# Batch 0 of a fused attention and gated MLP kernel in another order: loads, conversion, gate, outputs and attention parts

## Chip, cores, metric

One core of a Trainium2 chip. The metric is device time in microseconds (us), median of several executions. The engines are TensorE (PE), VectorE (DVE), ScalarE (ACT), and SyncE, which issues most of the DMAs.

## The reference

```python
# attention: x (8,8,512,64), state (8,8,32,64), float32, per batch and head
scores = x @ state.T / 8;  a  = softmax(scores);   xread = a @ state    # tokens read the state
scores2 = state @ x.T / 8; a2 = softmax(scores2);  sread = a2 @ x       # the state reads the tokens
# bridge: (batch, head, 544, 64) -> (4352, 512), then
h = x @ w_in             # w_in (512, 2048), float64 in memory
g = h * cos(h)
out = g @ w_out          # w_out (2048, 512), float64 in memory
```

## The kernel before

The weights come as float64 and are converted to float32 on the chip: 18 loads, each through two steps on DVE (`convert1`), two on ACT, two on DVE (`convert2`) and one on DVE (`convert3`). This happens in batch 0, beside its work. Later batches have nothing to convert.

For the tokens, `a @ state @ w_in` is regrouped. `products` computes state x w_in for a block of 512 columns (`sw`), and a tile's "hidden" matmul is `sw` x `aT` (128 of the 2048 columns for 512 tokens). The gate is a copy with a rounding bias (ACT), a subtraction (DVE), Abs and Sin (ACT) and a product (DVE). The "output" matmuls accumulate g x w_out in four PSUM tiles; the line `line` keeps them some tiles behind. All attention parts go through one PSUM tile, `at`. The schedule is manual: each engine gets its instructions in program order.

```python
st_src = state.rearrange("b (k j) n d -> j k n b d", j=2)
for k in range(NK):
    for j in range(2):
        queue = nc.sync if j == 0 else nc.scalar
        queue.dma_start(out=st[Ns * k:Ns * k + Ns, :, D * j:D * j + D], in_=st_src[j, k])
# ... (cut) weights: first 512 columns of w_in, then w_in and w_out in turn
for a, b in zip(rest_in, rest_out):
    loads += [a, b]
# ... (cut)
load_x(0); fetch(3); states()              # states(): turn the state on PE, copy on ACT and DVE
a0 = attn[0] = Attention(0)
a0.all_tokens(); a0.scores()               # turn x on PE, copy; scores into `at`
# ... (cut) softmax of batch 0 with the first two conversions between
for t in tiles(b):                         # 16 tiles a batch; conv = 3 + t.f in batch 0
    hidden(t)
    gate(t)                                # ACT q <- h
    if conv and t.f: convert1(conv + 1)
    gate2(t)                               # DVE q <- q, h
    if conv: convert2(conv)                # (first tile cut)
    gate3(t)                               # ACT Abs, Sin
    go()                                   # one attention part, if the slot has one
    line.append(t)
    if len(line) > 3: output(line.pop(0))
    gate4(t)                               # DVE g <- h, q
    if conv: convert3(conv)
    go()
```

## Time and profile before

| | before |
|---|---|
| median (first three runs) | 903.25 us |
| PE busy | 841.5 us, 93% of the span |
| PE without a gap | from 178.1 us (batch 1's first hidden matmul) |
| hidden 0 starts | 29.20 us |

From 178 us on PE has no hole.

### The profile page before, as it was taken

How to read it: one execution, taken by the hardware profiler on the slowest of the kernel's cores; microseconds unless marked ns; L12 is line 12 of the kernel's file. 1: busy time of each engine (PE TensorE's matmuls, PEld its weight loads, DVE VectorE, ACT ScalarE, POOL GpSimd, SP SyncE). 2: the span in 40 equal slices, each digit the busy share in tenths (PEclk: the TensorE clock that was granted, in tenths of full speed). 3: DMA queues.
4: the chain of work that ended last, by engine and by line, in shares of the span. 5: the costliest groups of instructions: out<-in, count | busy, mean ns of one | idle time of the engine just before them, and what ended most of it. 6: DMA issues, size and time to landing. Idle time of an engine off the chain costs nothing.

```text
span 901.1 us, 7084 instructions
## 1 busy us (share of the span) xinstructions
PE 841.5 (93%) x2720; PEld 385.2 (43%) x2720; DVE 356.7 (40%) x520; ACT 408.9 (45%) x631; POOL 0.7 (0%) x6
## 2 busy tenths in 40 slices
PE   3569867899999999999999999999999999999997
PEld 2134324244534453444444443445344534444664
DVE  4687885335322443245224522353225322222121
ACT  2546563355344634464344525453455344434332
POOL 0000000000000000000000000000000000000000
PEclk9689988999999999999999999999999999999999
DMA  6632630021000300030003000300010000000100
GB/s 163 186 141 96 184 140 1 0 70 24 1 1 23 71 0 1 1 93 1 0 1 93 1 0 1 91 4 1 1 47 1 0 1 23 24 0 1 47 1 23
DMA packets 45377, 35.05 MB, mean 39 GB/s; under 512 B 36384, under 2 KB 36384, under 8 KB 45344
## 3 DMA queue, kind: packets, MB, share of 16 engines
q1 hardware_dynamic: 44256, 34.35, 13.4%
q8 instruction: 21, 0.34, 0.2%
q10 hardware_dynamic: 1088, 0.26, 0.2%
q14 instruction: 12, 0.10, 0.0%
HBM read 25.69 MB, written 8.91 MB: 38 GB/s over the span
## 4 chain that ended last, share of the span: by engine, by line
PE 86%; DVE 7%; ACT 4%; issue 1%; DMA 0%; ACTq 0%; DVEq 0%
PE o L403 48%; PE h L373 28%; PE at L245 5%; PE at L311 3%; PE at L219 1%; DVE e L176 1%; ACT e L165 1%; ACT raw L166 1%; DVE w_in L189 1%; PE at L300 1%; DVE w_in L179 1%; ACT q L379 1%; ACT q L388 1%; DVE w_out L189 1%; DVE q L382 1%
## 5 line engine op out<-in xcount | busy, mean ns | idle before, releaser
L403 PE MATMUL o<-w_out,g 128*128 128x512 f32 x1088 | 495.3, 597 | 5.9 <-DVE w_out L189 5.9
L403 PEld LDWEIGHTS o<-w_out,g 128*128 128x128 f32 x1088 | 204.4, 192 | 249.3 <-issue 236.7
L373 PE MATMUL h<-aT,sw 128*128 128x512 f32 x512 | 250.9, 613 | 4.1 <-ACT sw L343 3.4
L382 DVE SCALAR_TENSOR_TENSOR q<-q,h 128x512 f32<-128x512 f32 (+1 forms) x144 | 94.3, 655 | 348.0 <-ACT q L379 348.0
L379 ACT ACTIVATE q<-h 128x512 f32<-128x512 f32 (+1 forms) x144 | 82.5, 573 | 276.1 <-PE h L373 276.1
L393 DVE TENSOR_TENSOR g<-h,q 128x512 f32<-128x512 f32 (+1 forms) x144 | 95.2, 661 | 158.9 <-ACT q L388 158.7
L373 PEld LDWEIGHTS h<-aT,sw 128*128 128x128 f32 x512 | 96.4, 195 | 128.3 <-issue 111.2
L387 ACT ACTIVATE q<-q 128x512 f32<-128x512 f32 (+1 forms) x144 | 87.2, 606 | 105.2 <-DVE q L382 105.2
L388 ACT ACTIVATE q<-q,halfpi 128x512 f32<-128x512 f32 (+1 forms) x144 | 100.5, 698 | 4.5
L245 PE MATMUL at<-w_in,stT 64*32 64x512 f32 (+1 forms) x528 | 41.6, 606 | 24.1 <-DVE w_in L189 12.2
L343 ACT COPY sw<-at 128x1024 f32<-128x1024 f32 (+1 forms) x33 | 32.3, 978 | 43.6 <-PE at L245 43.6
L311 PE MATMUL at<-x_b,a2T 128*128 128x256 f32 x128 | 32.0, 396 | 4.0 <-DVE a2T L303 4.0
L311 PEld LDWEIGHTS at<-x_b,a2T 128*128 128x128 f32 x128 | 25.3, 199 | 13.9 <-issue 6.5
L373 PE MATMUL h<-sT,w_in 128*128 128x256 f32 x128 | 30.2, 379 | 0.0
L245 PEld LDWEIGHTS at<-w_in,stT 64*32 64x32 f32 x528 | 6.8, 106 | 54.8 <-DVE w_in L189 17.8
L373 PEld LDWEIGHTS h<-sT,w_in 128*128 128x128 f32 x128 | 24.3, 190 | 10.1 <-issue 5.0
L409 ACT ACTIVATE ot<-o 128x512 f32<-128x512 f32 x34 | 19.4, 596 | 19.8 <-DMA out_dram<-ot 14.7
L165 ACT ACTIVATE e<-e,ebias 128x1024 int32<-128x1024 int32 (+1 forms) x18 | 18.9, 1051 | 11.4 <-DVE e L162 11.4
L219 PEld LDWEIGHTS at<-ident,x_b 128*128 128x128 f32 x112 | 13.8, 141 | 16.7 <-issue 12.0
L263 DVE STREAM_TRANSPOSE spread<-m 128x1024 f32<-128x1024 f32 x16 | 19.8, 1236 | 0.0
L176 DVE SCALAR_TENSOR_TENSOR e<-raw,e 128x1024 int32<-128x1024 int32 (+1 forms) x18 | 19.7, 1096 | 0.0
L226 ACT COPY xT<-at 128x512 f32<-128x512 f32 x28 | 16.0, 571 | 8.1 <-PE at L219 8.1
(49 smaller groups left out, 269.5 us busy)
## 6 DMA issues: line engine op xcount, KB each, us to landing
x_b<-in_x_dram SPq DMA_DIRECT2D x32, 256.0 KB, 4.7
raw<-in_moe_w_out_dram SPq DMA_DIRECT2D x8, 1024.0 KB, 4.8
out_dram<-ot SPq DMA_DIRECT2D x32, 256.0 KB, 2.2
raw<-in_moe_w_in_dram SPq DMA_DIRECT2D x6, 1024.0 KB, 5.2
raw<-in_moe_w_in_dram SPq DMA_DIRECT2D x4, 512.0 KB, 5.4
out_dram<-ot SPq DMA_DIRECT2D x8, 64.0 KB, 1.7
st<-in_state_dram ACTq DMA_DIRECT2D x4, 64.0 KB, 3.2
st<-in_state_dram SPq DMA_DIRECT2D x4, 64.0 KB, 3.0
```

Source lines behind the costliest of these rows:

```text
L165: nc.scalar.activation(e, e, func=ACTF.Relu, bias=ebias, scale=8.0)
L176: nc.vector.scalar_tensor_tensor(out=e, in0=raw[:, :, :, 1], scalar=-2 ** 31, in1=e, op0=ALU.bitwise_and, op1=ALU.bitwise_or)
L245: nc.tensor.matmul(out=at[Ns * k:Ns * k + Ns, j, 0:n], lhsT=w[D * j:D * j + D, self.b, Ns * k:Ns * k + Ns], rhs=r(slice(D * j, D * j + D), k),
L311: nc.tensor.matmul(out=at[:, 0, cols], lhsT=self.a2T[:, j, c, :], rhs=self.x_b[:, c].rearrange("p (k j) d -> p j k d", j=2)[:, j], start=( ...
L343: nc.scalar.copy(sw_of[self.b, nt][:, :, c0:c1], at[:, :, 0:c1 - c0])
L373: nc.tensor.matmul(out=t.hp, lhsT=t.lhs(i), rhs=t.rhs(i), start=(i == 0), stop=(i == t.kn - 1))
L379: nc.scalar.activation(t.q, t.hp, func=ACTF.Copy, bias=MAGIC)
L382: nc.vector.scalar_tensor_tensor(out=t.q, in0=t.q, scalar=MAGIC, in1=t.hp, op0=ALU.subtract, op1=ALU.subtract)
L387: nc.scalar.activation(t.q, t.q, func=ACTF.Abs)
L388: nc.scalar.activation(t.q, t.q, func=ACTF.Sin, bias=halfpi, scale=-TWO_PI)
L393: nc.vector.tensor_tensor(t.g[:, 0:t.n], t.hp, t.q, op=ALU.mult)
L403: nc.tensor.matmul(out=acc[i], lhsT=t.g[:, P * i:P * i + P], rhs=w_out[:, t.f, :], start=(t.f == 0), stop=(t.f == NF - 1))
```

## The change

The intent: let PE, which waits through most of batch 0, wait less. x's loads go first. w_in is converted ahead of w_out, so that each block of `products` is ready a tile earlier. Conversion steps go ahead of the gate within a tile. Outputs run four tiles behind. The parts by which the state reads the tokens (turns, reads) go into the middle slots, and three of batch 1's four product sets go into batch 1.

```diff
-    queue = nc.sync if j == 0 else nc.scalar
-    queue.dma_start(out=st[...], in_=st_src[j, k])
+    nc.scalar.dma_start(out=st[...], in_=st_src[j, k])      # after load_x(0) on nc.sync
@@ loads
-    for a, b in zip(rest_in, rest_out):
+    for a, b in zip(rest_in[1:], rest_out):                 # rest_in[0] put right behind the first four
@@ turn
-            nc.vector.tensor_copy(a2T[:, j], at[:, j])
+            nc.scalar.copy(a2T[:, j], at[:, j])
@@ start
-    states(); a0.all_tokens(); a0.scores()
+    a0.all_tokens(); states(); a0.scores()
     (exp2 and max2 behind norm1; the first products into output tiles instead of `at`)
@@ batch 0's slots (two a tile; P0, P1 products, L state half, E softmax half of batch 0 or 1)
+    slots0 = [[], [P0[0]], E1[0:1], E1[1:2], E1[2:3], E1[3:4], [P0[1]],
+              L0[0:1], L0[1:2], [], L0[2:3], L0[3:4], L0[4:5], [],
+              [P0[2]], L0[5:6], E1[4:5], E1[5:6], E1[6:7], E1[7:8], E1[8:9],
+              E1[9:10], [P0[3]], E1[10:11], E1[11:12], L1[0:1],
+              L1[1:2], [P1[0]], L1[2:3], L1[3:4], L1[4:5], L1[5:6]]
@@ tile
             hidden(t)
-            gate(t)
             if conv and t.f:
                 convert1(conv + 1)
+                convert2(conv)
+            gate(t)
             gate2(t)
-            if conv: convert2(conv)
+            if conv: convert3(conv)
             gate3(t)
             ...
-            if len(line) > 3:
+            if len(line) > 4:
                 output(line.pop(0))
             gate4(t)
-            if conv: convert3(conv)
```

(The g buffers grow from five to six.)

More of the change, by code (lines that the diff above doesn't have):

```diff
@@ L53 @@
     swp = ctx.enter_context(tc.tile_pool(name="swp", bufs=6))
-    gp = ctx.enter_context(tc.tile_pool(name="gp", bufs=5))
+    gp = ctx.enter_context(tc.tile_pool(name="gp", bufs=6))
     msb = ctx.enter_context(tc.tile_pool(name="msb", bufs=2))
@@ L76, with load_x @@
     make_identity(nc, ident)
+    x_t = {}
+    def load_x(b):
+        x_b = xin.tile([P, NC, H, D], F32, name="x_b")
+        src = x[b].rearrange("h (c p) d -> c p h d", p=P)
+        for c in range(NC):
+            nc.sync.dma_start(out=x_b[:, c], in_=src[c])
+        x_t[b] = x_b
+    load_x(0)
     st_src = state.rearrange("b (k j) n d -> j k n b d", j=2)
@@ L79 @@
         for j in range(2):
-            queue = nc.sync if j == 0 else nc.scalar
-            queue.dma_start(out=st[Ns * k:Ns * k + Ns, :, D * j:D * j + D],
-                            in_=st_src[j, k])
+            nc.scalar.dma_start(
+                out=st[Ns * k:Ns * k + Ns, :, D * j:D * j + D],
+                in_=st_src[j, k])
     at = aps.tile([P, 2, S], F32, name="at")
@@ L96, in states @@
                                     op0=ALU.mult)
-    x_t = {}
-    def load_x(b):
-        x_b = xin.tile([P, NC, H, D], F32, name="x_b")
-        src = x[b].rearrange("h (c p) d -> c p h d", p=P)
-        for c in range(NC):
-            nc.sync.dma_start(out=x_b[:, c], in_=src[c])
-        x_t[b] = x_b
     w_in = consts.tile([P, NK, Dff], F32)
@@ L129 @@
     rest_out = [out_load(f) for f in range(0, NF, 2)]
-    for a, b in zip(rest_in, rest_out):
+    for a, b in zip(rest_in[1:], rest_out):
         loads += [a, b]
-    loads += rest_out[len(rest_in):]
+    loads.insert(len(loads) - 2 * (len(rest_in) - 1), rest_in[0])
+    loads += rest_out[len(rest_in) - 1:]
     raws = {}
@@ L238, in all_tokens, with per_head @@
                     nc.vector.tensor_copy(self.xT[:, k], xp[k])
-        def per_head(self, w, r, n=S):
+        def per_head(self, w, r, n=S, to=None):
             for k in range(NK):
@@ L245, in per_head @@
                     nc.tensor.matmul(
-                        out=at[Ns * k:Ns * k + Ns, j, 0:n],
+                        out=(to[j] if to else at[:, j])[Ns * k:Ns * k + Ns,
+                                                        0:n],
                         lhsT=w[D * j:D * j + D, self.b, Ns * k:Ns * k + Ns],
@@ L276, in shift, with exp1, exp2 @@
             nc.vector.tensor_tensor(self.z1, at, self.spread, op=ALU.subtract)
-        def exps(self):
+        def exp1(self):
             nc.scalar.activation(self.z1, self.z1, func=ACTF.Exp)
+        def exp2(self):
             for j in range(2):
@@ L283, in exps @@
                                      accum_out=self.i2[:, j:j + 1])
+        def exps(self):
+            self.exp1()
+            self.exp2()
         def inverse(self, v):
@@ L302, in turn @@
                                     identity=ident)
-            nc.vector.tensor_copy(
-                self.a2T[:, j].rearrange("p c m -> p (c m)"), at[:, j])
+            nc.scalar.copy(self.a2T[:, j].rearrange("p c m -> p (c m)"),
+                           at[:, j])
         def reads(self, j):
@@ L343, in products, with first_products @@
             nc.scalar.copy(sw_of[self.b, nt][:, :, c0:c1], at[:, :, 0:c1 - c0])
+        def first_products(self, n):
+            to = [ops.tile([P, Dm], F32, name="o") for j in range(2)]
+            self.per_head(stT, lambda rows, k: w_in[rows, k, 0:n], n, to)
+            sw_of[self.b, 0] = swp.tile([P, 2, WC], F32, name="sw")
+            for j in range(2):
+                nc.scalar.copy(sw_of[self.b, 0][:, j, 0:n], to[j][:, 0:n])
         def scores1(self):
@@ L440, in tiles @@
             yield t
-    load_x(0)
     fetch(3)
-    states()
     a0 = attn[0] = Attention(0)
     a0.all_tokens()
+    states()
     a0.scores()
@@ L450 @@
     a0.max1()
+    a0.spread1()
+    a0.shift()
+    a0.exp1()
     convert2(0)
     convert3(0)
-    a0.spread1()
-    a0.shift()
-    a0.max2()
-    a0.exps()
+    a0.sums()
     convert1(1)
-    a0.sums()
     a0.spread1()
@@ L462 @@
     a0.norm1()
+    a0.first_products(HC)
+    a0.max2()
+    a0.exp2()
     load_x(1)
-    a0.products(0, 0, HC)
     convert1(2)
     convert1(3)
-    first = [lambda: a0.products(0, HC, WC)] + parts(0, PRODS[1:])
+    P0 = [lambda: a0.products(0, HC, WC)] + parts(0, PRODS[1:])
+    L0 = parts(0, LATE)
+    W1 = parts(1)
+    E1, L1, P1 = W1[:12], W1[12:18], W1[18:]
+    slots0 = [[], [P0[0]], E1[0:1], E1[1:2], E1[2:3], E1[3:4], [P0[1]],
[3 more added lines that the diff above has]
+              L1[1:2], [P1[0]], L1[2:3], L1[3:4], L1[4:5], L1[5:6]]
     line = []
@@ L471 @@
         work = parts(b + 1) if b + 1 < B else []
-        if b == 0:
-            late = parts(0, LATE)
-            work = ([None] + first[:1] + late[:5] + first[1:2] + late[5:]
-                    + work[:4] + [None] * 2 + first[2:3] + work[4:11]
-                    + first[3:] + work[11:])
-        n_slots, slot = 2 * NF, 0
-        n_done = 0
+        if b == 1:
+            work = P1[1:] + work
+        n_slots, slot, n_done = 2 * NF, 0, 0
         def go():
             nonlocal n_done, slot
+            if b == 0:
+                for part in slots0[slot]:
+                    part()
             slot += 1
             want = (len(work) * slot + n_slots - 1) // n_slots
-            if b == 0:
-                n = 3 * NF // 2
-                want = min(slot, n) + max(slot - n, 0) * (len(work) - n) // (
-                    n_slots - n)
-            while n_done < want:
-                if work[n_done]:
-                    work[n_done]()
+            while n_done < want and b > 0:
+                work[n_done]()
                 n_done += 1
@@ L508 @@
                     convert3(conv - 1)
-                convert2(conv)
+                    convert2(conv)
+                convert3(conv)
             gate3(t)
@@ L512 @@
             line.append(t)
-            if len(line) > 3:
+            if len(line) > 4:
                 output(line.pop(0))
             gate4(t)
-            if conv:
-                convert3(conv)
-                if t.f == 0:
-                    convert1(conv + 1)
+            if conv and t.f == 0:
+                convert1(conv + 1)
             go()
```

## The prediction

> **What bounds the kernel now.** I read the page's 40 slices first. TensorE (PE) is at 9 from slice 10 on; it is only in the first eight slices (22.5 us each, batch 0) that it is not.
>
> ```profile
> PE   3569867899999999999999999999999999999997
> ...
> DVE  4687885335322443245224522353225322222121
> ACT  2546563355344634464344525453455344434332
> ...
> PEclk9689988999999999999999999999999999999999
> ```
>
> Then the table of windows. To be seen: from 180 us on PE has no gap until the last microseconds, so the end is "when does PE become gapless" plus "how much matmul work is left then". Before that VectorE (DVE), which converts the weights from f64, is the fullest engine.
>
> ```profile
> 20.00:30.00 10.00, 2.96 (x17) 0.90 (x18) 9.70 (x16) 5.10 (x10) 0.00 (x0) 0.50 0.23 70
> 140.00:150.00 10.00, 4.42 (x17) 2.61 (x16) 10.00 (x13) 4.69 (x6) 0.00 (x0) 0.81 0.01 2
> 180.00:190.00 10.00, 10.00 (x34) 5.12 (x33) 2.76 (x4) 5.42 (x9) 0.00 (x0) 1.00 0.01 2
> 280.00:500.00 220.00, 220.00 (x717) 98.03 (x716) 78.06 (x112) 104.61 (x164) 0.00 (x0) 1.00 0.12 29
> ```
>
> Third, the chain in order of time, for one tile of batch 0. To be seen: ACT holds the gate's first copy (L379), then two conversion steps, then Abs and Sin, then the attention's copy; only then may PE transpose and run the next tile's "hidden" matmul. That loop is 6.8 us while a settled tile needs 1.72 (L373 x4) + 3.44 (L403 x8) = 5.16 us.
>
> ```profile
> 78.16 0.60 ACT q L379
> 78.76 1.04 ACT e L165
> 79.79 1.05 ACT raw L166
> 80.84 0.53 ACT q L387
> 81.39 0.72 ACT q L388
> 82.11 0.48 ACT xT L226
> 82.64 0.66 PE at L219 x4
> 83.30 1.73 PE h L373 x4
> ```
>
> Last, PE's waits: no single one is large, so no single removal can give much. (The chain names the rest: round trips between DVE, ACT and PE.)
>
> ```profile
> PE at L245 <- DVE w_in L189: 12.2, 6, 3.3
> PE at L245 <- ACT z L281: 8.3, 1, 8.3
> PE o L403 <- DVE w_out L189: 5.9, 4, 4.6
> PE at L300 <- DVE a2T L303: 5.2, 2, 3.7
> PE at L311 <- DVE a2T L303: 4.0, 1, 4.0
> ```
>
> **How much is lost now.** Batch 1's first hidden matmul starts at 178.1 us (timeline). Done by then, at warm durations: 16 hidden x 1.72 = 27.5; 13 outputs x 3.44 = 44.7; attention of batches 0 and 1, from its own rows (a set of products or scores 1.1, reads of one batch 3.4, turns 0.9, 16 transposes of x 1.8), about 25.3. Sum 97.5. So some 80.6 us are lost, 29.2 minus about 4 of them before tile 0. At most this can be won, and DVE's work forbids most of it.
>
> **What the Trainium skill says.** "TensorE: Matmul & The Clock Gate", Part 1: PE idles at half rate, and about 3.4 us of activity releases it. The trace agrees: granted clock 0.50 at 20 to 30 us, and the first hidden matmul takes 3.79 us against 1.72 later. The same page's note on queue depths calls ACT and DVE strict FIFO. The trace agrees: the z transposes at 43.30 end near 44.1, but their 0.6 us copy on DVE (L303) starts only at 47.05, behind the gate and two conversion steps. "ScalarE: Activation LUTs", section on ACT_TABLE_LOAD: about 1283 ns for a switch of set, plus a drain. The trace has the 1.28 us load; no 1.38 us drain is to be seen, the next activation follows at once.
>
> **The change, part by part.**
>
> *Start.* x now leads its queue (issued near 0.7 instead of 3.45 us), but state and x still share the DMA engines, which were full until about 10 us, and the state's two transpose halves come after x's copies on ACT and DVE. By trace durations the scores start at about 13.4 to 14.8 us (13.04 now). From there the order on DVE is shorter: max 1.25, spread 1.2, shift 1.23, conversion 0 1.83, sums 1.87, half of conversion 1 0.66, spread 1.25, conversion 1 1.83, so the first products can go 13.1 us after the scores, their copies end at 15.0, and hidden 0 starts 15.05 after the scores; now it is 29.20 - 13.04 = 16.16. Together 28.5 to 29.8 us: nothing won.
>
> *Order in a tile.* Now ACT runs L379, L165, L166, L387, L388; after, the two conversion steps come ahead of L379. Worked through from the start of a tile's first DVE step (pitches from the timeline: L162 and L163 0.6 each, L176, L179, L189 1.14 each, L382 and L393 0.6): ACT starts e at 0.73, raw ends 2.83, L379 until 3.45; DVE has finished its two conversion steps at 3.5, gate2 to 4.1, last conversion step to 5.25; ACT's Sin starts at 4.89, so gate4 runs 5.64 to 6.25. Period 6.25 us, DVE waiting only 0.4 of it. Attention pieces on DVE add to this.
>
> *w_in ahead of w_out.* Columns 512 to 1023 are ready after tile 2 instead of tile 3, the next two sets after 6 and 10. The products then stand in the first slot of tiles 3, 7, 11, beside the gate, and the 12.2 us of waits on L189 should go. The next hidden matmul still waits for ACT's 1.0 us copy of them.
>
> *Tiles 0 to 3.* With output delayed to four tiles, PE does nothing there but hidden matmuls and x's transposes of batch 1, so it stays mostly cold (3.4 us each). ACT's copy after Sin, transpose, copy and cold hidden make tiles 2 and 3 about 7.5 us. By this walk gate4 ends at 38.4, 47.3, 54.8, 62.3 us for tiles 0 to 3; now 38.1, 48.3, 56.2, 63.9. Little won.
>
> *Tiles 4 to 13.* Here it gains. DVE's work: 10 tiles x 5.94 (conversion 4.65 + gate 1.29) = 59.4, keep 1.5, batch 1's softmax 9.0 (1.25 + 1.14 + 1.15 + 1.21 + 1.8 + 1.24 + 1.22), sum 69.9. Waits on top: 0.4 in most tiles, 3; a cold hidden 4 behind turn 0, 2; tile 5, where PE has 8.6 us (hidden, two halves of reads, output), 2; Exp's table load ahead of the sums with no conversion step left to fill the gap, 2. So gate4 of tile 13 ends near 62.3 + 69.9 + 9 = 141 us (now 149). a2T's copies move from DVE to ACT right behind Sin, which removes most of the L303 waits (9.2 us).
>
> *From there.* PE is gapless from batch 1's first products, placed after tile 13's Sin, about 140.5 us. Done by then: 14 hidden 24.1 + 10 outputs 34.4 + attention 17.3 (as above, without batch 1's reads 3.4, three product sets 3.3 and small parts) = 75.8. Loss 140.5 - 75.8 = 64.7; 1 us more for late waits: 65.7. Saved: 80.6 - 65.7 = 14.9 us, and 903.25 - 14.9 = 888 us. The longer line and batch 1's three extra products only move work that PE has to do anyway, into a stretch without gaps.
>
> **Rivals.** (1) *DVE floor reached*: PE is never late and warms early. Tiles 4 to 13 would lose none of the 9 us, and tiles 1 to 3 perhaps 3 less: 888 - 12 = 876. For it: 82% to 100% DVE already at 110 to 130 us. Against: `at` is one PSUM tile for all attention parts, each waiting for the copy of the previous one on a strict FIFO. (2) *A new wait takes the old one's place*: conversion ahead of L379 delays the gate whenever a weight load lands late (DVE waited 0.8 us for one at 40.68), and ACT now also carries the a2T copies; hidden 12 and 14 stand behind products whose copies come after Sin. Half the gain would go: 895. (3) *Only moved*: the gain in batch 0 comes back in batch 1, where four outputs and three products are left over: if PE were counted by tiles (hidden of batch 1 at 157 against 178) one would say 21 us, but 6.7 us of this is deferred work. That is already subtracted. A full loss is unlikely, as steady batches have been gapless with 22 attention parts, and 25 fit the 32 slots.
>
> **Range and chances.** The centre is 888. Rival 1 bounds it below near 876, rival 2 above near 895; a miss of S by 1.5 us or a cold clock in tiles 4 and 5 adds 2 to 4. I take 878 to 898. The 2% line is 885.2, about 3 us under the centre with a spread of about 8: faster 0.35, same 0.63, slower 0.02.
>
> **What would show it.** Right: hidden 0 still at 28 to 30 us; granted clock near 0.5 in much of 35 to 65 us; tile period about 6.3 us where no attention stands; the waits of the products on the conversion under 3 us; the a2T waits gone from DVE; PE gapless from about 140 us; batch 1's first hidden near 157. Wrong: if hidden 0 starts before 26 us or tiles 0 to 3 take under 30 us, the gain exceeds 20 us; if PE gets gapless only after 150 us, or steady batches show new PE gaps (evictions meeting the first output), it is under 8.

## The result, and the profile after

| | before | after |
|---|---|---|
| median, 6 runs each | 903.08 us (902.40 to 905.52) | 892.72 us (891.85 to 897.28) |
| hidden 0 starts | 29.20 us | 34.54 us |
| tile 0's gate product to tile 3's | 25.8 us | 23.1 us |
| tile 3's to tile 13's | 85.2 us | 75.5 us |
| batch 1's first hidden matmul | 178.09 us | 159.78 us |

The ratio is 0.9886 (95% interval 0.9861 to 0.9911): within 2%, 10.3 us less. A ratio is the mean time of one kernel's fast runs over that of the other's of the same rounds, so it is not quite the ratio of the medians quoted.

The 40 slices after. To be seen: DVE starts at 1 in its first slice (4 before): the start is later. It then runs fuller, and PE's lasting 9 begins one slice earlier: with slice 8, and with slice 9 before.

```profile
PE   3369968999999999999999999999999999999997
...
DVE  1888986234313431352224422442235222222121
```

Next the chain of work that ended last, in order of time, from the changed kernel's start (start, duration, what). To be seen: it leads through two of the state's loads, one behind the other, up to 14.55 us; before it the state was on the chip at 5.97 us. The scores (L248) start at 19.72 us instead of 13.04. First the two lines of the timeline of the kernel before, then the chain.

```profile
5.97 1.09 PE L90 MATMUL at<-ident,st 128*128 128x128 f32 x4 [5.97 <-DMA st<-in_state_dram]
...
13.04 1.97 PE L245 MATMUL at<-xT,stS 64*32 64x512 f32 x16
```

```profile
2.53 4.64 DMA st<-in_state_dram
7.19 7.37 DMA st<-in_state_dram
14.55 0.14 issue
14.69 1.10 PE at L102 x4
...
19.72 2.04 PE at L248 x16
```

One tile in the timeline (start, duration, engine, line, operation): batch 0's tile 5. To be seen: ACT's conversion steps (L168, L169) now run ahead of the gate's copy (L397), and DVE comes from one tile's first step (L165) to the next in 80.89 - 74.67 = 6.22 us, with 0.32 us idle ahead of the product.

```profile
74.67 0.68 DVE L165 TENSOR_SCALAR e<-raw 128x1024 int32<-128x1024 int32 x1
75.39 1.15 ACT L168 ACTIVATE e<-e,ebias 128x1024 int32<-128x1024 int32 x1 [0.89 <-DVE e L165]
76.44 1.16 ACT L169 ACTIVATE raw<-raw 128x1024 f32<-128x1024 uint32 x1
77.50 0.58 ACT L397 ACTIVATE q<-h 128x512 f32<-128x512 f32 x1
...
80.28 0.69 DVE L411 TENSOR_TENSOR g<-h,q 128x512 f32<-128x512 f32 x1 [0.32 <-ACT q L406]
80.89 0.68 DVE L165 TENSOR_SCALAR e<-raw 128x1024 int32<-128x1024 int32 x1
```

PE's waits (total, times, longest). To be seen: outputs no longer wait for w_out, and the a2T waits shrink from 9.2 to 2.4 us. What is left on w_in is the two halves of block 0 (10.2 into `o`, 4.7 into `at`), not blocks 1 to 3. Of the 12.2 us before, 8.1 were block 0's too (2.99 + 3.34 + 1.77 in the timeline) and 4.1 those of blocks 1 to 3 (0.79 + 1.40 + 1.88).

```profile
PE o L248 <- DVE w_in L192: 10.2, 2, 6.0
PE at L248 <- ACT z L287: 6.6, 1, 6.6
...
PE at L248 <- DVE w_in L192: 4.7, 2, 3.9
...
PE at L248 <- ACT a2T L313: 2.4, 1, 2.4
```

The sum: batch 1's first hidden matmul is 18.3 us earlier. One more output (3.4 us) and three more product sets (3.3 us) are then still to do. And there is a new hole: near 187 us, where the fourth turn of batch 1's successor is copied only behind four evictions on ACT, of which the third waits for its buffer's store.

```profile
187.56 1.28 ACT L427 ACTIVATE ot<-o 128x512 f32<-128x512 f32 x2 [1.68 <-DMA out_dram<-ot]
...
189.36 1.09 PE L248 MATMUL at<-xT,stS 64*32 64x512 f32 x16 [1.69 <-ACT xT L229]
```

18.3 - 3.4 - 3.3 - 1.7 = 9.9 us; the spans of the two profiled runs differ by 901.1 - 891.4 = 9.7.

So batch 0 is 23.7 us shorter from hidden 0 on (from 148.9 to 125.2 us up to batch 1's first hidden; 6.7 of it is deferred work), and the start lost 5.3 of it. The experiments ask, first, what made the start late, and second, which part made the gain.

### The profile page after: what moved, and what is told of

Same layout as the page of the kernel before. It is cut to its first block, busy times and chain, and to the rows that moved or that the text cites. A ratio compares the mean times of both kernels' runs of the same rounds, so it can differ in the third digit from the quotient of the medians.

```text
span 891.4 us, 7090 instructions
## 1 busy us (share of the span) xinstructions
PE 833.2 (93%) x2720; PEld 382.2 (43%) x2720; DVE 346.3 (39%) x504; ACT 417.8 (47%) x648; POOL 0.7 (0%) x6
## 4 chain that ended last, share of the span: by engine, by line
PE 85%; DVE 7%; ACT 4%; DMA 2%; issue 1%; ACTq 0%; DVEq 0%
PE o L421 49%; PE h L391 26%; PE at L248 4%; PE at L321 3%; DMA st<-in_state_dram 1%; PE at L222 1%; DVE e L179 1%; DVE q L400 1%; PE at L310 1%; ACT q L406 1%; DVE w_out L182 1%; ACT q L405 1%; DVE e L165 1%; DVE w_in L182 1%; ACT e L168 1%
## 5 line engine op out<-in xcount | busy, mean ns | idle before, releaser
L397 ACT ACTIVATE q<-h 128x512 f32<-128x512 f32 (+1 forms) x144 | 82.4, 573 | 239.5 <-PE h L391 239.5
L248 PE MATMUL at<-w_in,stT 64*32 64x512 f32 (+1 forms) x512 | 36.8, 616 | 13.7 <-ACT z L287 6.6
L168 ACT ACTIVATE e<-e,ebias 128x1024 int32<-128x1024 int32 (+1 forms) x18 | 19.0, 1054 | 22.0 <-DVE e L165 22.0
L222 PE MATMUL at<-ident,x_b 128*128 128x128 f32 x112 | 18.0, 286 | 6.2 <-ACT xT L229 6.2
L248 PEld LDWEIGHTS at<-w_in,stT 64*32 64x32 f32 x512 | 6.1, 106 | 39.8 <-issue 17.6
```

The lines of the kernel that those rows point to most:

```text
L222: nc.tensor.transpose(out=out[:, P * c:P * c + P], in_=self.x_b[:, c, 2 * k:2 * k + 2, :], identity=ident)
L248: nc.tensor.matmul(out=(to[j] if to else at[:, j])[Ns * k:Ns * k + Ns, 0:n], lhsT=w[D * j:D * j + D, self.b, Ns * k:Ns * k + Ns], rhs=r(sl ...
L397: nc.scalar.activation(t.q, t.hp, func=ACTF.Copy, bias=MAGIC)
```

## The experiments

Every run gave a correct result, and each was timed in five rounds beside the kernel before on its chip. "Against after" below is the difference of the two ratios to the kernel before, times 903 us; each ratio has an interval of about 0.002, or 1.8 us, either way, that of the changed kernel 2.3 us, so a difference in the last column has up to 2.9 us either way.

| run | edit | median us | ratio to before | against after, us |
|---|---|---|---|---|
| e1 | after, state's loads first | 888.27 | 0.9835 | -4.6 |
| e2 | after, state's loads and turns first | 885.00 | 0.9794 | -8.3 |
| e3 | after, state's loads behind x on one queue | 890.00 | 0.9845 | -3.7 |
| e4 | before, with the new start | 909.87 | 1.0070 | |
| e5 | after, gate ahead of conversion | 898.19 | 0.9927 | +3.7 |
| e6 | after, old order of the weights | 901.72 | 0.9970 | +7.6 |
| e7 | after, outputs three tiles behind | 900.84 | 0.9961 | +6.8 |
| e8 | after, old slots | 899.81 | 0.9947 | +5.5 |
| e9 | after, a2T copies on DVE | 892.97 | 0.9892 | +0.5 |
| e10 | e2, batch 1's slots changed | 888.36 | 0.9823 | -5.7 |
| e11 | e10, two parts of batch 0 moved | 882.33 | 0.9769 | -10.6 |
| e12 | before, w_in first and four tiles | 899.73 | 0.9954 | |

### The start: e1 to e4

The theory: the state lands late because of where its loads stand. The rival: it is the order of turns and copies.

e1:

```diff
+    (state loads, j == 0 on nc.sync, j == 1 on nc.scalar, as before)
     load_x(0)                         # now behind them
     a0.all_tokens(); states()         # unchanged
```

> The changed kernel with only the state's eight loads put back ahead of x, half on each queue; TensorE still turns x before the state. Theory A (the state's last load landed at 14.6 us because x and the first weights share the 16 DMA engines with it): the state lands near 6 us, x near 11 us, TensorE turns x until about 12.5, and the state's turns and their copies follow in the 5.0 us that they took: scores at about 17 (19.7 in the changed kernel), hidden 0 near 32, time near 890. Theory B (the order of turns and copies on TensorE, ACT and DVE is what delays, not the landing): no change, scores at 19 to 20, time 892 to 893.

Scores at 16.48 us, hidden 0 at 31.30, 888.27 us. Theory A holds, and the order of turns has a share too: with the state there at 6 us, its turns still wait behind x's.

e2, in addition:

```diff
-    a0.all_tokens(); states()
+    states(); a0.all_tokens()
```

> As the previous one, and the state's turns ahead of x's again, so the whole start is that of the kernel before. Theory A: scores at about 13.0 as in the kernel before, hidden 0 at about 28 (15 us after the scores), 6.5 us earlier than in the changed kernel; all of it reaches the end: time 886 to 887. Rival (the later stages absorb it, since DVE and not the start bounds batch 0): hidden 0 early but under 3 us of it left at the end, time above 890.

The timeline of e2 for PE: the state's turns (L101) start at 5.90, x's (L221) at 9.30, the scores (L247) at 12.96.

```profile
5.90 1.08 PE L101 MATMUL at<-ident,st 128*128 128x128 f32 x4 [5.90 <-DMA st<-in_state_dram]
...
9.30 3.62 PE L221 MATMUL o<-ident,x_b 128*128 128x128 f32 x16
12.96 1.97 PE L247 MATMUL at<-xT,stS 64*32 64x512 f32 x16
```

Hidden 0 starts at 27.71 us, 6.8 earlier than in the changed kernel, and the time is 8.3 us less: nothing was absorbed. The rest matches tile 14: from its hidden matmul to that of tile 15 it is 8.7 us here and 10.4 in the changed kernel, where that matmul ran cold, that is at the lower clock (3.39 us for its four passes, 1.98 here).

e3:

```diff
-            nc.scalar.dma_start(out=st[...], in_=st_src[j, k])
+            nc.sync.dma_start(out=st[...], in_=st_src[j, k])     # still after load_x(0)
```

> The changed kernel with the state's loads on x's own queue, behind x and ahead of the weights. Theory A (sharing with the weights): with the weights behind it the state lands at about 10 to 11 us instead of 14.6, scores at about 15.5 to 16, time near 889. Rival (issuing eight loads takes long wherever they are issued, or their small packets are slow whoever shares): the state lands at 13 us or later, time 891 to 893; the later weights may then delay the first conversion, which would show as a DVE wait on a weight load before 25 us.

The state's first turn starts at 11.09 us, the scores at 16.11, hidden 0 at 30.92, and the time is 3.7 us less. So being on the same queue as x, ahead of the weights, beats a queue of its own beside them. Two things differ. In the changed kernel the last four state loads are issued only as earlier loads finish: the instruction list shows each waiting for the semaphore (the counter that tells a load's end) of one, which the program gives it again, and ACT's eight issues stretch from 0.74 to 7.6 us (four took 1.92 before). And those late ones then share the DMA engines with three weight loads that SyncE issued from 4.65 us on; the last landed 7.37 us after its issue at 7.19, where the fastest needed 3.6. The trace of e3 parts the two: there the last state load is issued even later, at 8.10 us, still ahead of the weights, and lands 2.7 us after that. So a late issue alone does not make the state this late; what is left is the transfers beside it.

e4 (the kernel before):

```diff
-    (state loads on two queues); load_x(0); fetch(3); states(); a0.all_tokens()
+    load_x(0); (state loads on nc.scalar); fetch(3); a0.all_tokens(); states()
```

> The kernel before with only the start of the changed one: x ahead, state on ACT's queue alone, x turned before the state. Theory A: scores at 19.7 instead of 13.04, hidden 0 near 35.9, time 903 + 6.7 = about 909.7. Rival (the later part absorbs it): under 905.

Scores at 19.21, hidden 0 at 35.42, 6.2 us later than before; the time is 0.7% more, 6.3 us. From both sides the new start costs what it delays. It is the part of the change that harms. (From the scores to hidden 0 it is 16.2 us here and 14.8 in the changed kernel, so the new order of the first softmax and products is worth about 1.4 us there; no run undid it alone.)

### The parts that gain: e5 to e9

e5:

```diff
             hidden(t)
-            if conv and t.f: convert1(conv + 1); convert2(conv)
             gate(t)
+            if conv and t.f: convert1(conv + 1)
             gate2(t)
+            if conv and t.f: convert2(conv)
-            if conv: convert3(conv)
             gate3(t)
             ...
             gate4(t)
+            if conv: convert3(conv)
```

> The changed kernel with the kernel before's order inside a batch-0 tile: the gate's first copy ahead of the conversion steps on ACT, its subtraction ahead of the two conversion steps on DVE, the last conversion step behind the gate's product. Theory (this order is what shortens the tile): the waits of DVE for Sin and of TensorE for ACT's copies return, tiles 4 to 13 grow from 75.5 us by 3 to 6 us, time 895 to 899. Rival (DVE has the same work either way, and the gain of tiles 4 to 13 comes from the slots and the output line): within 1.5 us of the changed kernel, 891 to 894.

3.7 us more by the ratios, within the expected times. Tiles 4 to 13 take 78.2 us instead of 75.5, 2.7 more and just under the expected 3 to 6, and tile 0's product to tile 3's takes 27.6 instead of 23.1 (hidden 0 came 0.7 us earlier in this run). So the order is worth something, but not where the theory had it. In tiles that run undisturbed the period, from one gate product to the next, is no longer with the old order. Tile 5, whose attention part is matmuls alone, takes 6.25 us here (first two lines) and 6.22 in the changed kernel; tile 13 takes 6.08 and 6.20; and in the kernel before tile 7, with no attention part, took 6.09 (last two lines).

```profile
79.61 0.69 DVE L411 TENSOR_TENSOR g<-h,q 128x512 f32<-128x512 f32 x1 [0.40 <-ACT q L406]
85.86 0.69 DVE L411 TENSOR_TENSOR g<-h,q 128x512 f32<-128x512 f32 x1 [0.24 <-ACT q L406]
```

```profile
89.05 0.69 DVE L393 TENSOR_TENSOR g<-h,q 128x512 f32<-128x512 f32 x1 [0.41 <-ACT q L388]
95.14 0.69 DVE L393 TENSOR_TENSOR g<-h,q 128x512 f32<-128x512 f32 x1
```

What e5 loses lies in tiles 1 to 4 (7.0 us together) and 6 (1.4), which have attention work on ACT or DVE; tile 11 is 1.4 us shorter. And hidden 3 and 4 ran cold in e5 (3.62 us each against 1.88), so how much of the 7.0 us is the order's own stays open.

e6:

```diff
-    for a, b in zip(rest_in[1:], rest_out):
+    for a, b in zip(rest_in, rest_out):
```

> The changed kernel with the weights in the old order (w_in and w_out alternating from the start); everything else stays, the products in tiles 3, 7 and 11 now wait for the conversion step of their own tile. Theory (the products' result is copied only after that tile's Sin, so the 12 us of waits that this part removes were mostly not on the path): within 2 us of the changed kernel, 892 to 894.5, though several us of waits of the products on the conversion are back. Rival (my prediction's wording: the 12.2 us of waits go): 897 or more.

7.6 us more: my theory falls, the rival holds. The timeline of e6 from the end of tile 7 shows what I had left out. To be seen: the second half of the products waits 3.90 us for its conversion; behind it on PE stands an output, which takes 5.36 us now (3.43 in a gapless stretch); and only behind that comes hidden 8, at 103.18.

```profile
96.01 1.93 PE L247 MATMUL at<-w_in,stT 64*32 64x512 f32 x8 [3.90 <-DVE w_in L191]
...
97.87 5.36 PE L420 MATMUL o<-w_out,g 128*128 128x512 f32 x8
...
103.18 1.88 PE L390 MATMUL h<-aT,sw 128*128 128x512 f32 x4
```

The products' copy stood behind Sin in any case, but hidden 8 does not wait for the copy alone. It waits for all that stands ahead of it on PE, and the late products push the output. From tile 7's gate product to tile 8's it is 12.9 us here and 7.1 in the changed kernel.

e7:

```diff
-            if len(line) > 4:
+            if len(line) > 3:           # and five g buffers
```

> The changed kernel with outputs three tiles behind instead of four, and five g buffers. Theory: the first output then stands in tile 3 behind the conversion of the w_out part that it reads and ahead of hidden 4, on a cold TensorE, so hidden 4 comes some 5 us later; 3.4 us of output work is done earlier in exchange: 893 to 897. Rival (TensorE has room for it): 3.4 us less, 889.5.

6.8 us more, above the expected range by the median and by the ratio (899.5 us). One line of PE's waits, absent in the changed kernel, tells why:

```profile
PE o L421 <- DVE w_out L192: 17.0, 5, 4.8
```

Every second output now stands in the tile that converts its weights, and the next hidden matmul stands behind it. The theory had named only the first of these five waits, which is 1.53 us. Batch 1's first hidden matmul comes 10.5 us later, for 3.4 us of work done earlier.

e8:

```diff
-    slots0 = [...]; batch 1: work = P1[1:] + work
+    work = ([None] + first[:1] + late[:5] + first[1:2] + late[5:] + work[:4] + [None] * 2
+            + first[2:3] + work[4:11] + first[3:] + work[11:])      # as in the kernel before
```

> The changed kernel with the attention's parts in batch 0's old slots: the state half of batch 0 in tiles 1 to 3 instead of 3 to 7, x's turns of batch 1 after it, all products of batch 1 within batch 0. Theory: the state half fills an idle TensorE early but then collides with the products (one PSUM tile for both), and at the end the last three products of batch 1 and the reads wait for each other as in the kernel before: 896 to 900. Rival (slots hardly matter, DVE bounds): 891 to 894.

5.5 us more. In its waits PE stands 8.5 us ahead of hidden matmuls for the products' copy (2.0 in the changed kernel), 7.9 for a2T and 4.8 for the state's result. The theory holds.

e9:

```diff
-            nc.scalar.copy(a2T[:, j], at[:, j])
+            nc.vector.tensor_copy(a2T[:, j], at[:, j])
```

> The changed kernel with the four a2T copies of batches 0 and 1 (and of all later ones) on DVE again. Theory (DVE is full in tiles 4 to 13, ACT is not): four copies of 0.6 us each in DVE's full stretch, and in two of them DVE also waits about 1 us for the turn on TensorE: time 3 to 5 us over the changed kernel, 896 to 898. Rival (the copies only fill holes on either engine): within 1.5 us, 891.5 to 894.

0.5 us more, nothing that can be told from zero. The theory falls: with the turns in other slots and the conversion order changed, DVE reaches these copies soon enough. The a2T waits are 2.6 us with these copies on DVE and 2.4 on ACT, while the old slots bring back 7.9 (e8): they went because of the slots, not of the engine.

### Do the parts add up? e12

The kernel before, with two parts:

```diff
-    for a, b in zip(rest_in, rest_out):
+    for a, b in zip(rest_in[1:], rest_out):     # rest_in[0] behind the first four
-            if len(line) > 3:
+            if len(line) > 4:                   # and six g buffers
```

> The kernel before with only two parts of the change, which need each other: w_in converted ahead of w_out, and outputs four tiles behind (six g buffers). Undoing either alone cost 8 to 9 us in the changed kernel. Theory (the parts are worth what they are worth only together, because each undone part puts a wait ahead of an output on the in-order TensorE): alone, the 12.2 us of the products' waits on w_in and the 5.9 us of the outputs' on w_out mostly go, but the old slots and the old order in the tile keep their own waits, and 3.4 us of output work is deferred: 897 to 901. Rival (the parts add up): 903 - 8.5 = 894.5 or less.

4.2 us less by the ratio, although undoing either alone cost 7 to 8. The outputs' waits for w_out fall from 5.9 to 3.1 us and the products' on w_in from 12.2 to 7.7, but those for the state's result grow from 2.0 to 5.9 and those of hidden matmuls for the products' copy from 3.4 to 5.2. So the two parts, 14.4 us when their costs of undoing are added (7.6 + 6.8), bring 4.2 without the others: they are shares of one schedule, not terms of a sum. (The costs of undoing in e5 to e8 add to 23.6 us, against 10.3 + 8.3 = 18.6 for all parts without the start, but the changed kernel's interval of 2.3 us counts four times in that sum, so this surplus alone is not clear of noise.)

### Towards a better version: e10, e11

e10, on e2, against the hole near 187 us (near 181 in e2):

```diff
-            work = P1[1:] + work
+            work = P1[1:2] + work[:9] + P1[2:] + work[9:]
```

> The state loaded and turned first (as in e2), and in batch 1 one deferred product ahead of x's turns and two behind the exponentials, so that the last copy of x's turn no longer stands behind four evictions on ACT. Theory: TensorE's 1.69 us wait for ACT xT near 181 us goes and nothing comes in its place: 885.0 - 1.7 = 883.3. Rival (the wait moves to the evictions' own accumulators or to the products' copies): 885.

888.36 us (884.54 to 889.06). The wait for ACT xT ahead of the scores is gone, but PE's waits of e10 show another in its place. In e2 the wait for z came once (6.6); now there is a second of 1.4 us, where the next product stands right behind the exponentials.

```profile
PE at L247 <- ACT z L286: 8.0, 2, 6.6
```

So the wait moved, as the rival said, but to a place that it did not name. The median is even 3.4 us above e2, above both expectations. I do not lay that to the edit: batch 0 is the same program in both, and hidden 4 starts at the same time, but takes 1.88 us in e2 (first line) and 3.62 here (second).

```profile
62.48 1.88 PE L390 MATMUL h<-aT,sw 128*128 128x512 f32 x4
```

```profile
62.45 3.62 PE L390 MATMUL h<-aT,sw 128*128 128x512 f32 x4
```

So hidden 5 started at 70.58 us here and at 68.07 in e2, with a granted clock of 0.90 against 1.00 between 62 and 90 us; e10's own runs spread over 4.5 us. Why the clock fell so in one run and not in the other I leave open.

e11, on e10:

```diff
-              E1[9:10], [P0[3]], E1[10:11], E1[11:12], L1[0:1],
-              L1[1:2], [P1[0]],
+              [], E1[9:10] + [P0[3]], [P1[0]] + E1[10:11], E1[11:12],
+              L1[0:1], L1[1:2], [],
```

> As e10, and in batch 0 the sums of batch 1 go half a tile later (behind tile 11's conversion, so that DVE works while ACT loads the Exp table), and the first product set of batch 1 goes from behind the second turn of tile 13 to behind the products of tile 11. Theory: DVE's waits of 1.7 us for Exp and 1.6 us for Sin shrink to about 1 us together, and hidden 14 no longer waits for the a2T copy (2.4 us): 3 to 5 us less than e10, 878 to 880. Rival (the product's copy on ACT delays the conversion of tile 12 as much as it saves): 883.

882.33 us, 4.9 less than e10 in the same rounds, but above the expected 878 to 880. DVE's wait for Exp ahead of the sums (1.7 us) is gone, and so is PE's for a2T ahead of hidden 14 (2.4), which starts at 133.78 us (138.11 in e2). In the profiled runs part of the difference is that e10's cold hidden 4 did not come again (1.88 us here); against e2 the ratios give 2.3 us, on another chip and with about 2 us either way, and the profiled spans 4.2. This version is 2.3% under the kernel before and beats the changed kernel by about 10 us.

## Why the prediction was right or wrong

The range (878 to 898) held, and so did "within 2%"; the centre was 4.7 us too low.

- *Start: wrong.* "By trace durations the scores start at about 13.4 to 14.8 us": 19.72. The step that failed is the one ahead of it: I let eight state loads finish beside x by about 8 to 10 us because the DMA engines had been full until then, and counted neither their late issue nor the weights behind x. From the scores to hidden 0 I had 15.05 us, and the trace has 14.82, so the rest of this term was right. e2 and e4 show the size: the start costs 6 to 8 us, of which the loads alone are 4.6 (e1). That is larger than the whole miss.
- *Order in a tile: right in the number, but the order did not make it.* 6.25 us predicted, 6.22 measured, with the predicted short wait ahead of gate4 (0.32). But an undisturbed tile took 6.09 us in the kernel before and 6.25 in e5, with the old order. The loop of 6.8 us that I set against it was read in a tile with a turn and a copy of x in it. What the order gains, 3.7 us by e5, it gains in other tiles, 1 to 4 above all.
- *Tiles 0 to 3: right in size, half right in cause.* From tile 0's gate4 to tile 3's I had 23.9 us; 23.1. Hidden 0 to 2 ran cold as foreseen (3.78, 3.78 and 3.62 us), but hidden 3 took 1.88 us. The mean granted clock was 0.77 between 35 and 65 us, not near 0.5; that mean has the first 5 us at 1.00, where hidden 0 took its 3.78.
- *Tiles 4 to 13: mechanism right, waits mis-sized.* 78.7 us predicted (of them 9 for waits), 75.5 measured, so about 6 for waits. The cold hidden 4 that I put at 2 us took 1.88 us in all and cost nothing. The wait for Exp was there as foreseen (1.7 us).
- *w_in ahead of w_out: right in direction, wrong in size.* I had all 12.2 us of waits go, and under 3 left. Only 4.1 of them were those of blocks 1 to 3, and these went; block 0's grew from 8.1 to 14.9 us (10.2 + 4.7), which this part could not reach. That waits of blocks 1 to 3 lie on the path, by way of the output behind them, is shown by e6, which brings 9.2 us of them into the changed kernel.
- *a2T on ACT: wrong.* The waits shrank, but e9 shows that the copies' engine had no share in it that can be told from zero.
- *Gapless point and deferred work: right.* Gapless but for one hole from 143.1 us (140.5 predicted); batch 1's first hidden at 159.78 (157); deferred work 6.7 us as counted; late waits 1.7 us (1 predicted).
- *Rivals.* The first was partly right: DVE's waits were fewer than I had summed. The second came true in a place that it did not name, a transfer at the start. The third is why 18.3 us became 9.9.

Of the signs that I named, the tile's period (6.22), the a2T waits gone from DVE, the gapless point (143.1) and batch 1's first hidden (159.78) came near; hidden 0 at 28 to 30 us (34.54), a clock near 0.5 (0.77) and under 3 us of waits on the conversion (14.9) did not.

The range held in part by luck, for two misses pull against each other: the start lost 5.4 us against the middle of my 28.5 to 29.8 (and tile 0 another 0.8), while from tile 0's product to tile 13's it took 4.0 less (0.8 and 3.2). What is left of that is about the 2.6 us by which PE becomes gapless late. With 1.7 us for hidden 14, which ran cold, and the 0.7 us that the hole near 187 us has over what I had allowed, this makes 5.0 of the 5.2 us between the 14.9 us predicted and the 9.7 between the profiled spans. One reading was a little off too: DVE was the fullest engine up to 160 us (114.1 us busy, PE 109.5), not up to 180 (121.7 and 126.1).

On the Trainium skill: "TensorE: Matmul & The Clock Gate", Part 1, says that the two clock states hang on a free-running window and so vary from run to run. e2 and e10 fit that: the same batch 0 with a granted clock of 1.00 and 0.90 between 62 and 90 us, though one profile of each, on two chips, does not show the reason.

## What to carry to other kernels

A load that heads the longest chain goes ahead of the large ones, even where it is small; look at when it lands, not at when it is issued. (Whether it must also be spread over two queues no run tested alone.) A gain that comes to the predicted number still needs the experiment that takes its cause away: the tile's period was the same with the old order. On an in-order engine ask what stands behind an instruction that waits, for that, and not the wait's own consumer, may be on the path. Count what a schedule defers before you count how much earlier its next phase begins.

## What the Trainium skill lacked or had wrong

- "DMA: Bandwidth & Descriptors", section "Issuing engines are not separate DMA queues", says that issuing from several engines saves only issue time, usually small beside the transfer. For one load the trace agrees: 0.32 to 0.63 us to issue, 3.6 to 7.4 to land. But eight loads of 64 KB on ACT's queue alone took from 0.74 to 7.6 us to issue, since four of them waited for earlier ones, and landed at 14.6 us; spread over two queues and ahead of x, they were there at 5.9 us. What small loads lose beside large ones has no figure in that section: the same loads landed 2.3 to 3.5 us after their issue in e2, where they led.
- "ScalarE: Activation LUTs", section "What ACT_TABLE_LOAD costs", gives about 2.66 us for a switch of set, of which 1.38 is a drain. In the changed kernel Sin ends at 117.32 us, the load runs from 117.34 for 1.28 us, and Exp starts at 118.63: 1.31 us in all, and no drain to be seen.
